# A planner that counts TensorE's instructions: gaps between pieces of 256, and a new order of every queue

## The chip, the cores and the metric

The kernel runs on one core of a Trainium2 chip. Its time is the device time of one execution in microseconds, here the median of several runs. The kernel is written with a manual schedule: the order in which each engine's instructions are emitted is the order in which that engine runs them, and engines wait for each other through semaphores.

## The reference

Two branches over 2,048 tokens of width 512 are mixed by a gate per token. Branch A is causal attention with 32 heads of 16 in four segments of 512 tokens, plus a compressed memory that each segment reads before its keys and values are added to it; branch B is a ReLU-gated feed-forward layer with an inner width of 1,792.

```python
def _A_ref(x, wq, wk, wv, wo, beta):
    ...
    for s in range(N):                       # four segments of 512 tokens
        logits = jnp.einsum('bhqd,bhkd->bhqk', qs, ks) * scale + mask
        p = _softmax(logits, axis=-1)
        a_dot = jnp.einsum('bhqk,bhkd->bhqd', p, vs)
        pq = phi(qs)
        a_mem = einsum(pq, M) / (einsum(pq, z) + 1e-06)
        outs.append(g * a_mem + (1.0 - g) * a_dot)
        M, z = M + einsum(phi(ks), vs), z + sum(phi(ks))
    return o @ wo
...
def _B_ref(x, W_gate, W_up, W_down):
    h = relu(x @ W_gate) * (x @ W_up)
    return h @ W_down
...
g = _sigmoid((x * gate_w).sum(-1, keepdims=True))
return g * a + (1 - g) * b
```

Inputs and the output are bfloat16.

## The kernel before

The work is cut into some 1,100 steps. A step is a function that emits a few instructions on one engine (or a pair of engines to choose from), with a list of the steps it comes after, a cost in microseconds, and whether it takes or gives back one of four PSUM banks (`rb`). `Plan.add` (line 125) records a step. The order of each queue is written out by hand in the list `ORDER` (line 41): each number is a step's place times five plus the engine, so it says both which engine does the step and where it stands in that engine's queue. `Plan.lay_out` (line 139) walks the five queues, always taking the queue whose next step can start first by the plan's own costs. That decides which PSUM bank a step gets and the order of emission across engines; the order within an engine is the one in `ORDER`. On TensorE it adds `SWITCH` = 0.094 us whenever the mode of tiles changes.

The steps that the text speaks of, by the letters of their names (then come the segment and other numbers):

- Q, K, V: projections of a segment, four wide matmuls each (L479, L522; for the first segment's values L505). QC, KC, VC move them out of PSUM on ScalarE or VectorE.
- QK (L738): one of nine fills of the score tile `sp` for two groups of four heads; 16 matmuls on tiles of the array, 8 for the smallest kind. EX (L749): ScalarE's exp of the whole tile into one of 11 buffers `E`; the next QK can start only when it is done, and an EX into a buffer that is still to be read waits for its reader. MK (L759): GpSimd masks the diagonal blocks of that buffer.
- PV (L786): the product with the values for one group of heads, 64 matmuls with a weight load each, once all masks of its parts are done; it takes two PSUM banks. TA, N, TB normalise and transpose the result on VectorE; OA adds the memory's part to it, on VectorE or GpSimd.
- MZ (L635): the memory's update after a segment, 64 matmuls with a weight load each; MA and MB turn it into the next memory matrix (MB on VectorE or GpSimd). MR (L681): reading the memory.
- G and U (L897): gate and up projections of one of 14 slices, four wide matmuls each. R (ReLU) and H (product) take them out.
- D and DB (L931; L855 for the last rows), W (L944; L863): the down projection in two halves of seven matmuls and the output projection into the same bank; OS scales and ST stores.
- XT, KX, MX, VS: DMA transposes and copies on SyncE's queue, beside the loads of the weights.

So TensorE's stream mixes wide matmuls (128 x 512, one weight load per matmul) with blocks of PV, MZ and QK whose matmuls use parts of the array and follow each other much faster.

Of the kernel before, what the change touches and what calls it, by code (L numbers as in the profile page):

```python
# [14 lines left out]
D = 512  # L15
# [17 lines left out]
NWARM = 19  # L33
# [68 lines left out]
]  # L102
T0, TU, SPAN, PEN_D, PEN_A, PEN_P = 19.0, 15.6, 4.1, -23.0, 150.0, 146.0


PORT = {'TG', 'RN', 'RC', 'OA', 'KO', 'MB', 'MQ', 'MN', 'GS', 'PQ', 'PK', 'N1', 'N2', 'N3', 'NM'}
PIECE = {'MK': 0.445, 'TL': 0.22, 'ZE': 0.24, 'YL': 0.22, 'MB': 0.3}


# [899 lines left out]
```

## Time and profile before

| | |
|---|---|
| median of 3 runs | 273.73 us (272.71 to 275.43) |
| the profiled execution | 274.39 us, of which 272.7 us from the first to the last instruction (the span) |
| mean granted TensorE clock | 0.994 |
| TensorE busy | 260.6 us (96%), 3,296 matmuls in the records |
| ScalarE, VectorE, GpSimd busy | 187.4, 184.9, 148.8 us |
| chain that ended last | TensorE 95%, "issue" 3%, DMA 1% |

The page gives busy times as a union per engine; "issue" is time in which the engine waited for nothing that the profile shows. The chain of work that ended last follows the end of the kernel back from releaser to releaser, and the answer in order of time lists its pieces as start, duration and what ran (L numbers are lines of the kernel before). The queue named q8 in the section on DMA queues carries instructions. Some matmul records are missing from a trace; the weight loads are complete.

### The profile page before, as it was taken

To read this page: it belongs to the slowest core of one execution; us is meant where nothing else is said; L and a number is where in the kernel's file an instruction comes from. 1 tells how busy PE (TensorE), PEld (TensorE's weight loads), DVE (VectorE), ACT (ScalarE), POOL (GpSimd) and SP (SyncE) were. 2 spreads that over 40 slices of the span, in tenths; PEclk is the share of its full clock that TensorE was granted. 3 is DMA by queue.
4 is the path that set the end of the run, shared out by engine and by line. 5 is a ranking of instruction groups with operands and counts; after the bars stand their busy time and mean duration, and the time that the engine had idled before them with its cause. 6 is when DMAs were issued, how large, how long until landed. Compare 5 with 4: busy or idle time off the path is not lost.

```text
span 272.7 us, 7949 instructions
## 1 busy us (share of the span) xinstructions
PE 260.6 (96%) x3296; PEld 124.0 (45%) x3337; DVE 184.9 (68%) x457; ACT 187.4 (69%) x179; POOL 148.8 (55%) x326
## 2 busy tenths in 40 slices
PE   8999997999899999999899997999999999999995
PEld 5444444444444544443443553544544444445463
DVE  1493685799965769768883657975695449567931
ACT  3989975679667797778576794797576576785001
POOL 7056866357889435375876555388177435343200
PEclk9999999799999999999999999999999999999999
DMA  6998346017201410000722320000100100011201
GB/s 197 286 290 211 67 149 219 4 30 93 24 19 41 117 22 2 2 19 0 121 46 60 60 59 4 19 4 18 27 2 4 59 22 2 19 22 22 19 20 59
DMA packets 33422, 16.77 MB, mean 61 GB/s; under 512 B 20074, under 2 KB 33386, under 8 KB 33386
## 3 DMA queue, kind: packets, MB, share of 16 engines
q1 hardware_dynamic: 33098, 16.00, 25.2%
q8 instruction: 26, 0.43, 0.7%
q10 hardware_dynamic: 288, 0.26, 0.3%
q14 instruction: 10, 0.08, 0.1%
HBM read 8.26 MB, written 2.10 MB: 38 GB/s over the span
## 4 chain that ended last, share of the span: by engine, by line
PE 95%; issue 3%; DMA 1%; DVE 0%; DVEq 0%
PE rb L897 37%; PE rb L931 17%; PE rb L479 10%; PE sp L738 9%; PE rb L786 7%; PE rb L944 5%; PE rb L522 4%; PE rb L505 2%; PE rb L681 1%; PE rb L855 1%; DMA xT<-in_A_x_dram 1%; PE rb L635 1%; PE rb L392 1%; PE rb L863 0%; DVE rg L874 0%
## 5 line engine op out<-in xcount | busy, mean ns | idle before, releaser
L759 POOL TENSOR_SCALAR_AFFINE_SELECT E<-E 64x256 bf16<-64x256 bf16 x256 | 113.5, 443 | 100.0 <-ACT E L749 88.3
L749 ACT ACTIVATE E<-sp 128x2048 bf16<-128x2048 f32 x72 | 135.2, 1878 | 39.6 <-PE sp L738 37.8
L897 PE MATMUL rb<-xT,wg_sb 128*128 128x512 bf16 x214 | 56.2, 387 | 0.7 <-issue 0.2
L897 PE MATMUL rb<-xT,wu_sb 128*128 128x512 bf16 x211 | 54.7, 380 | 0.6
L916 DVE TENSOR_TENSOR hT<-rb,rg 128x512 bf16<-128x512 f32 x56 | 38.0, 685 | 17.3 <-PE rb L897 13.4
L931 PE MATMUL rb<-wd_sb,hT 128*128 128x512 bf16 x201 | 48.0, 380 | 0.7 <-issue 0.3
L897 PEld LDWEIGHTS <-wg_sb 128*128 128x128 bf16 x224 | 20.9, 100 | 25.0 <-issue 5.3
L738 PE MATMUL sp<-QT,KTo 32*64 32x512 bf16 (+7 forms) x512 | 30.3, 295 | 1.7 <-issue 1.7
L897 PEld LDWEIGHTS <-wu_sb 128*128 128x128 bf16 x224 | 20.5, 98 | 24.1 <-issue 3.3
L738 PE MATMUL sp<-QT,KT 16*64 16x512 bf16 (+7 forms) x512 | 30.6, 295 | 0.0
L931 PEld LDWEIGHTS <-hT 128*128 128x128 bf16 x210 | 19.6, 98 | 23.2 <-issue 2.1
L909 ACT ACTIVATE rg<-rb 128x512 bf16<-128x512 f32 x34 | 20.0, 596 | 10.7 <-PE rb L897 5.9
L804 DVE STREAM_TRANSPOSE tA<-rb 128x512 f32<-128x512 f32 x32 | 21.2, 693 | 7.5 <-PE rb L786 7.3
L738 PEld LDWEIGHTS <-KT 16*64 16x64 bf16 x512 | 10.6, 102 | 31.4 <-issue 30.5
L911 DVE TENSOR_SCALAR rg<-rb 128x512 bf16<-128x512 f32 x22 | 15.1, 686 | 8.0 <-PE rb L897 6.9
L786 PE MATMUL rb<-E,Vs 64*32 64x448 bf16 (+7 forms) x512 | 18.6, 284 | 1.0 <-issue 1.0
L786 PE MATMUL rb<-E,Vp 64*32 64x448 bf16 (+7 forms) x512 | 17.9, 284 | 1.1 <-issue 1.1
L479 PE MATMUL rb<-xT,wq_sb 128*128 128x512 bf16 x61 | 16.2, 381 | 0.2
L479 PE MATMUL rb<-xT,wk_sb 128*128 128x512 bf16 x61 | 15.5, 380 | 0.1
L944 PE MATMUL rb<-wo_sb,oT 128*128 128x512 bf16 x57 | 14.5, 380 | 0.2
L522 PE MATMUL rb<-wv_sb,xT 128*128 128x256 bf16 (+1 forms) x96 | 14.5, 277 | 0.1
L955 DVE TENSOR_SCALAR osb<-rb,ngcol 128x512 bf16<-128x512 f32 x8 | 6.0, 750 | 12.6 <-PE rb L944 12.6
(99 smaller groups left out, 295.9 us busy)
## 6 DMA issues: line engine op xcount, KB each, us to landing
out_dram<-osb SPq DMA_DIRECT2D x15, 128.0 KB, 1.8
wd_sb<-in_B_W_down_dram SPq DMA_DIRECT2D x1, 1792.0 KB
wg_sb<-in_B_W_gate_dram SPq DMA_DIRECT2D x3, 512.0 KB, 6.2
wu_sb<-in_B_W_up_dram SPq DMA_DIRECT2D x3, 512.0 KB, 7.0
Vs<-Vp SPq DMA_DIRECT2D x8, 144.0 KB, 2.6
wk_sb<-in_A_wk_dram SPq DMA_DIRECT2D x2, 256.0 KB, 4.2
wq_sb<-in_A_wq_dram SPq DMA_DIRECT2D x2, 256.0 KB, 5.7
wo_sb<-in_A_wo_dram SPq DMA_DIRECT2D x1, 512.0 KB, 8.3
```

Source lines behind the costliest of these rows:

```text
L479: nc.tensor.matmul(rb[s.bank][:], lhsT=w[:, ci, c * P:(c + 1) * P], rhs=xT[i][:, ci, :], start=(ci == 0), stop=(ci == NC - 1))
L522: nc.tensor.matmul(rb[s.bank][:, 0:n], lhsT=xT[i][:, ci, t * P:(t + 1) * P], rhs=wv_sb[:, ci, h * D // 2:h * D // 2 + n], start=(ci == 0), ...
L738: nc.tensor.matmul(sp[64 * h:64 * h + 64, j, off:off + m], lhsT=kt[32 * j:hi, c0 + w, 64 * ck:64 * ck + 64], rhs=QT[i][32 * j:hi, c0 + w, ...
L749: nc.scalar.activation(Er[n % NE][:], sp[:], ACT.Exp, scale=SCALE)
L759: nc.gpsimd.affine_select(out=v, in_=v, compare_op=ALU.is_ge, fill=0.0, base=0, pattern=[[0, 4], [1, 64]], channel_multiplier=-1)
L786: nc.tensor.matmul(rb[s.banks[h]][32 * j:32 * j + 32, q0:q0 + m], lhsT=v[64 * h:64 * h + 64, ck // 2, o:o + 32], rhs=Er[(base + f) % NE][6 ...
L804: nc.vector.transpose(tA[k].rearrange("p b w -> p (b w)"), rb[a.banks[r]][:])
L897: nc.tensor.matmul(rb[s.bank][:], lhsT=w[:, ci, fv * P:(fv + 1) * P], rhs=xT[i][:, ci, :], start=(ci == 0), stop=(ci == NC - 1))
L909: nc.scalar.activation(rgb[k][:], rb[a.bank][:], ACT.Relu)
L916: nc.vector.tensor_tensor(hT[:, fv, :], rb[a.bank][:], rgb[k][:], ALU.mult)
L931: nc.tensor.matmul(rb[b][:], lhsT=hT[:, fv, lc:lc + P], rhs=wd_sb[:, fv, :], start=(fv == 0), stop=False)
L944: nc.tensor.matmul(rb[hold.bank][:], lhsT=oT[i][:, ci, lc:lc + P], rhs=wo_sb[:, ci, :], start=False, stop=(ci == NC - 1))
```

## The change

Each step gets a count of the instructions that it puts on TensorE. `lay_out` adds them up along TensorE's queue. At a first edge of 186 and every 256 behind it, the step that crosses the edge is stretched so that it is crossed no sooner than 5.0 us behind the moment noted for the edge ahead; that moment is when the stream was 12 instructions ahead of that edge, or 5.0 us behind the one before, if that is later. This acts only on the plan's own clock: no instruction is added for it. `ORDER` is replaced as a whole, for all five queues. The steps themselves, their tiles and their dependences are as before.

The diff without the body of `ORDER`:

```diff
 ORDER = [
...
-    135, 81, 79, 140, 160, 150, 146, 170, 166, 157, 350, 176, 375, 380, 385, 390, 355, 396, 190, 180, 360, 197, 365,
+    135, 81, 79, 140, 150, 170, 146, 160, 157, 176, 350, 167, 355, 375, 360, 365, 380, 372, 190, 180, 385, 197, 390,
...
 PORT = {'TG', 'RN', 'RC', 'OA', 'KO', 'MB', 'MQ', 'MN', 'GS', 'PQ', 'PK', 'N1', 'N2', 'N3', 'NM'}
+CODE = {'WM': 2 * NWARM, 'XP': 4, 'VI': 2, 'YP': 4, 'D': 14, 'DB': 14, 'PV': 128, 'MZ': 96}
+PAGE, PAGE0, AHEAD, FETCH = 256, 186, 12, 5.0
 PIECE = {'MK': 0.445, 'TL': 0.22, 'ZE': 0.24, 'YL': 0.22, 'MB': 0.3}
...
     def add(self, name, engines, emit, after=(), prio=0.0, lat=0.15, take=False, give=None, which=None,
-            mode="full"):
+            mode="full", code=8):
...
+        s.code = CODE.get(kind, code)
...
         gp, lock, mode, order = (0.0, 0.0, 99.0), 0.0, "full", []
+        code, edge, asked, ask = 0, PAGE0, -99.0, 0.0
...
             if e == "PE":
                 cost += SWITCH if s.mode != mode else 0.0
                 mode = s.mode
+                for i in (edge - AHEAD, edge):
+                    if code <= i < code + s.code:
+                        t = now + cost * (i - code) / s.code
+                        if i < edge:
+                            ask = t
+                        else:
+                            cost += max(0.0, asked + FETCH - t)
+                            asked, edge = max(ask, asked + FETCH), edge + PAGE
+                code += s.code
...
             mr = add(f"MR{seg}{q}", {"PE": 0.061 * len(ks)}, mrv, after=d["PQ"] + st[seg - 1]["mb"], prio=want + 4.0 * q,
-                     take=True, lat=0.25)
+                     take=True, lat=0.25, code=2 * len(ks))
...
-            a = add(f"QK{seg}{c0}{f}", {"PE": 0.262}, qk, mode="rows",
+            a = add(f"QK{seg}{c0}{f}", {"PE": 0.262}, qk, mode="rows", code=16 * len(whole[f]),
                     after=[x for w in us for x in (d["Q"][c0 + w], d["KO"][c0 + w], d["K"][c0 + w])] + fills[-1:],
                     prio=tu - 20.0, lat=0.25)
```

In the new order of TensorE every one of the 357 steps is still there, on the same engine; 317 stand at another place, the farthest 64 steps away. Of ScalarE's 178 steps 140 stay on it. In sum ScalarE has three ReLUs less and two copies, one scaling of keys and one OS more; one MB and one minimum (MN, MQ) go from GpSimd to VectorE, two OA from VectorE to GpSimd. Around the densest code the two orders read as follows (before, then after):

```
QK021 PV00 PV01 QK022             QK022 PV00 PV01 G0_13 QK023 MZ0 U0_13
QK100 MZ0 PV02 PV03 QK101         K21 PV02 PV03 QK100 D01
QK120 PV10 PV11 G1_3 QK121        QK121 PV10 PV11 MZ1 QK122
QK200 MZ1 PV12 PV13 QK201         QK200 PV12 PV13 QK201
QK221 PV20 PV21 MZ2 QK222         QK221 PV20 PV21 MZ2 QK222
QK301 PV22 PV23 QK302             QK301 PV22 PV23 QK302
QK320 PV30 PV31 G3_1 QK321        QK321 PV30 PV31 G3_2 QK322
U3_13 PV32 PV33 U3_12 D30         G3_11 PV32 PV33 U3_11 D31
```

On SyncE's queue the first gate and up pieces go out as gate 0, gate 1, up 0, up 1 instead of gate 0, up 0, gate 1, gate 2; the transposes, copies and stores behind them are moved by at most ten places.

118 rows, old and new, of the table ORDER are left out of this document.

## The prediction

> **What bounds the kernel now.** I read the page first: sections 1, 2, 3 and 4, then the chain of work that ended last in order of time, then single stretches.
>
> ```profile
> span 272.7 us, 7949 instructions
> PE 260.6 (96%) x3296; PEld 124.0 (45%) x3337; DVE 184.9 (68%) x457; ACT 187.4 (69%) x179; POOL 148.8 (55%) x326
> PEclk9999999799999999999999999999999999999999
> q8 instruction: 26, 0.43, 0.7%
> PE 95%; issue 3%; DMA 1%; DVE 0%; DVEq 0%
> ```
>
> TensorE is busy for 260.6 of 272.7 us and carries 95% of the chain; no other engine passes 69%. So only two things can shorten the kernel: TensorE's idle time, 12.1 us, and the time at a lower clock (the single 7 in the clock row). The chain shows where most of the idle time lies:
>
> ```profile
> 43.12 2.19 PE rb L786 x128
> 45.50 1.69 issue
> 47.18 0.42 PE sp L738 x15
> ...
> 68.09 0.62 PE rb L635 x64
> 68.71 2.15 PE rb L786 x125
> 70.86 0.97 issue
> 71.83 0.39 PE rb L786 x3
> ...
> 129.77 0.61 PE rb L635 x64
> 130.38 1.20 PE rb L786 x68
> 131.59 1.08 issue
> 132.67 1.14 PE rb L786 x55
> ...
> 161.11 2.16 PE rb L786 x128
> 163.28 0.59 PE rb L635 x63
> 163.86 1.44 issue
> 165.30 0.18 PE rb L635
> ```
>
> There are four gaps in which TensorE waits for nothing that the profile shows: 1.69 + 0.97 + 1.08 + 1.44 = 5.18 us. All lie inside or just behind blocks of PV (L786) and MZ (L635), the densest code there is: 64 matmuls and 64 weight loads, 128 instructions, in 1.1 us or 0.6 us. Counted in the program's own order of TensorE's instructions, what waits is number 963, 1731, 3266 (a weight load) or 3267, and 4291. These lie 768, 1536 and 1024 apart, that is 3, 6 and 4 times 256, and queue q8 moved 0.43 MB in 26 pieces, which is 6,684 instructions cut into pieces of about 256. So I read the gaps as waits for the next piece of code, with edges at 195 + 256k.
>
> **How long a piece must last.** From the edge before each gap to its end: the two PVs of the first begin 3 instructions ahead of edge 707, so 43.15 to 47.18 = 4.0 us. Edge 1475 lies 2 matmuls ahead of the end of MZ: 68.69 to 71.83 = 3.1. Edge 3011 lies 9 matmuls into MZ: 129.86 to 132.67 = 2.8. Edge 4035 lies halfway through the two PVs' row: 162.19 to 165.30 = 3.1. Two pieces went by faster without a gap worth the name:
>
> ```profile
> 100.93 0.36 PE sp L738 x16
> 101.29 2.19 PE rb L786 x127
> 103.48 0.32 PE rb L897
> ...
> 195.28 0.35 PE sp L738 x16
> 195.63 1.94 PE rb L786 x119
> 197.58 0.01 issue
> ```
>
> Their edges (2243 and 4803) lie about halfway through a QK (L738), and they lasted 2.4 and 2.1 us. In the stretch 99.0 to 102.7 the only DMA traffic is one q8 piece, in the third of 40 slices, near 99.2: ahead of the edge.
>
> ```profile
> GB/s 0 0 177 0 0 0 0 0 0 0 0 0 0 0 0 0 0 0 0 0 0 0 0 0 0 0 0 0 0 0 0 0 0 0 0 0 0 0 0 0
> q8 instruction: 1, 0.02, 1.6%
> ```
>
> So code is asked for early where the instruction stream runs ahead of the array, and not where the edge lies deep in dense code. I take 3.1 us for such edges, with 2.1 (no gap) and 4.0 as ends.
>
> The first gap has a second price, seen in three stretches (columns: us; busy of PE, PEld, DVE, ACT, POOL; clock; DMA):
>
> ```profile
> 45.00:47.70 2.70, 1.01 (x33) 0.41 (x19) 1.07 (x5) 0.10 (x2) 2.11 (x5) 1.00 0.00 1
> 47.70:51.20 3.50, 3.28 (x11) 1.41 (x10) 2.32 (x5) 2.44 (x2) 1.41 (x4) 0.51 0.02 5
> 51.20:56.00 4.80, 4.75 (x47) 2.26 (x47) 4.18 (x12) 3.54 (x3) 1.05 (x3) 1.00 0.01 2
> ```
>
> Behind it the granted clock is 0.51 for 3.5 us, so about 0.49 x 3.5 = 1.7 us are lost; behind the gaps of 1.44, 1.08 and 0.97 us it is not. [...]
>
> **The change, part by part.** Two rows more of the chain in order of time, for the durations used here:
>
> ```profile
> 26.62 0.87 PE rb L897 x4
> 28.36 0.36 PE sp L738 x16
> ```
>
> The counting itself runs when the program is written and adds no instruction. What reaches the chip is a new order of the five queues. TensorE's 3,337 matmuls and loads are the same; 151 changes between tile modes become 152, about 0.1 us by the first matmul behind one (0.32 us at 103.48 against 0.87/4 = 0.22). So the price lies in where the edges now fall.
>
> The plan counts 96 instructions for an MZ. The code loops over 4 x 4 x 4 = 64 matmuls, each with its load, and the rows agree (three MZs):
>
> ```profile
> L635 PE MATMUL rb<-Vp,pK 128*32 128x34 bf16 x192 | 2.2, 183 | 1.4 <-issue 1.4
> L635 PEld LDWEIGHTS <-pK 128*32 128x32 bf16 x192 | 1.7, 93 | 0.8 <-issue 0.8
> ```
>
> That is 128, so behind each MZ the plan's edges lie 32 instructions later against the real ones. Its first edge (186, counted from the first warm-up load, number 3 in the program) stands 6 ahead of mine; behind the first MZ it is 26 late, then about 58, then about 90. The distance that the plan keeps is kept at the wrong places for most of the run. The blocks stay: all eight pairs of PVs are still adjacent, MZ1 now follows PV10 and PV11, MZ2 still follows PV20 and PV21; only MZ0 now stands apart from any PV.
>
> I price the pieces of the new order by rows: a PV matmul 2.19/128 = 0.0171 us, an MZ 0.61, a QK of 16 matmuls 0.36, a wide matmul 0.216 (and 0.1 more behind a QK).
>
> Edge 2499 (48 PV matmuls, MZ1, QK): 0.82 + 0.61 + 0.36 = 1.79 us, so a gap of 3.1 - 1.8 = 1.3. Edge 4035 (73 of PV, 55 of MZ2): 1.25 + 0.52 = 1.77, gap 1.3. Edge 4803 (122 of PV, 6 of QK), whose edge lies just inside the first PV as at 707: 2.09 + 0.13 = 2.22, gap 0.9. Edge 1475 (109 of PV, QK, 3 of the down-projection): 1.87 + 0.36 + 0.65 = 2.88, gap 0.2. Edge 5571 (112 of PV, 4 wide, 12 of QK): 3.2, none. Edge 707 (5 wide, QK, 107 of PV): 3.3, none. All others last over 5 us. Sum 3.7 us against 5.18: a gain of 1.5. Ends: at 2.8 a piece 1.0 + 1.0 + 0.6 = 2.6; at 4.0, 2.2 + 2.2 + 1.8 + 1.1 + 0.8 + 0.7 = 8.8.
>
> Clock: the new gaps of 1.3 us are nearest to 1.44, which had no dip, yet their upper end is beyond 1.69. I take half a dip, a gain of 0.85, ends 0 and 1.7.
>
> Waits from the new order: 317 of TensorE's 357 steps stand elsewhere, and nothing in the trace prices that. TensorE's idle time apart from the gaps is 12.1 - 5.2 = 6.9 us, of which about 4.1 lie ahead of its first and behind its last matmul; 2.7 are spread. This could vanish (-2.7) or double (+2.7). I take +0.5, near zero, because the tightest loop has no less room than before: QK needs the exp of the QK ahead.
>
> ```profile
> L749 ACT ACTIVATE E<-sp 128x2048 bf16<-128x2048 f32 x72 | 135.2, 1878 | 39.6 <-PE sp L738 37.8
> PEld L738 <- ACT E L749: 0.4, 1, 0.4
> ```
>
> TensorE waited for an exp once, 0.4 us, and by my count the new order's QKs are still at least 2.5 us apart against an exp of 1.88. PV00 and PV01 move behind QK022, whose exp overwrites the E buffer that PV00 reads. That exp waits for PV00 (1.1 us), and the next QK for the exp: 0.36 + 1.1 + 0.3 + 1.88 = 3.6 us behind QK022's start, where TensorE has 0.36 + 2.19 + 0.97 = 3.5 us of other work; a wait of 0.1 at most.
>
> The other queues: in sum three ReLUs go from ScalarE to VectorE and four small steps back, one MB and one minimum go from GpSimd to VectorE, two OA the other way; all on engines that are busy for 55 to 69%; where that cover is gone, such a step costs TensorE at most its own length. On SyncE one 512 KB gate piece is issued ahead of the first up piece. At the 290 GB/s of the page's third slice that is 1.8 us later for U0_0, which two gate projections and a QK now precede (2 x 0.97 + 0.36 = 2.3); hidden, 1.8 if not. VS and the transposes move by at most ten places.
>
> ```profile
> GB/s 197 286 290 211 67 149 219 4 30 93 24 19 41 117 22 2 2 19 0 121 46 60 60 59 4 19 4 18 27 2 4 59 22 2 19 22 22 19 20 59
> ```
>
> Sum against the profiled execution, 274.39 us (0.66 above the median 273.73; span 272.7): 274.39 - 5.18 + 3.7 - 0.85 + 0.5 = 272.56, about 272.5.
>
> **The rivals.** First, the gaps shrink to those in the blocks with MZ and no dip follows: the streams run ahead at 4803 and 1475 as they did at 2243. 274.39 - 5.18 + 2.6 - 1.7 = 270.1, with nothing for other waits. For it: two of before's six short pieces had no gap. Against it: edge 4803 now lies behind the PV's own waits for two banks.
>
> Second, the change does all it says: no gap, no dip, 274.39 - 5.18 - 1.7 = 267.5. Against it: the miscount of MZ, and five pieces priced under 3.2 us.
>
> Third, slower: pieces of code arrive at the longest interval, 4.0 us, at all six edges: 274.39 - 5.18 + 8.8 + 0.5 = 278.5. It decides by 1% (over 276.5) once the gaps sum to about 6.8, an interval of some 3.7 us at all six. For it: 4.0 was measured at the edge most like the new 4803. Against it: three of the four were 2.8 to 3.1.
>
> Fourth, the gaps are not code at all but belong to the blocks, and stay: 273.7. [...] Against it: the spacing of the gaps in multiples of 256.
>
> **How the numbers follow.** My forecast has 0.50, the fourth rival 0.05, the first 0.20, the second 0.08, the slower one 0.17. A difference under 1% (271.0 to 276.5) can hardly be told from none by a measurement of this kernel. Faster: 0.20 + 0.08 + 0.02 from the forecast's lower edge = 0.30; slower 0.17; within 0.53. The range leaves out the second rival and half of the slower one: 269.2 to 277.0; the forecast's own is 271.0 to 275.5.
>
> **What would show it.** Right: gaps put down to issue ahead of instructions 2755 and 4291, each 1.0 to 2.2 us, a smaller one at 5059, none at 963; still about 26 pieces in q8; TensorE's busy time within 1 us of 260. Wrong: no gap behind MZ1 or MZ2 (pieces are asked for earlier than I think), TensorE waiting for ScalarE, VectorE or a DMA for more than 2 us in all (the new order's own waits), or gaps at instructions that are not 195 + 256k.

## The result and the profile after

The new order took 270.55 us (median of six runs, 270.51 to 271.35) against 273.15 for the kernel before (median of six, 272.71 to 275.43); the ratio is 0.9896, with an interval of 0.9861 to 0.9931. So it is faster, by about 1%. The page of its profiled execution, which took 270.55 us:

```profile
span 268.8 us, 8007 instructions
...
PE 261.6 (97%) x3337; PEld 124.0 (46%) x3337; DVE 187.4 (70%) x460; ACT 188.6 (70%) x180; POOL 146.3 (54%) x322
...
PEclk9999999999999999999999999999999999999999
...
q8 instruction: 26, 0.43, 0.7%
...
PE 90%; DVE 5%; issue 1%; DMA 1%; ACT 1%; DVEq 0%
```

The 7 in the clock row is gone, "issue" in the chain fell from 3% to 1%, and the number of code pieces is as before (26 in q8). The chain in order of time, at the places that the prediction named (lines are those of the kernel after: 799 is PV, 648 is MZ, 751 is QK, 910 a gate or up projection):

```profile
44.96 2.23 PE rb L799 x128
47.20 0.97 PE rb L910 x4
...
102.44 1.15 PE rb L799 x64
...
105.84 0.89 DVE o L828 x2
106.74 0.04 issue
106.78 1.90 PE rb L910 x8
...
160.05 2.16 PE rb L799 x128
162.21 0.51 PE rb L648 x53
162.72 0.87 issue
163.59 0.25 PE rb L648 x10
...
189.35 2.19 PE rb L799 x128
191.54 0.21 PE sp L751 x5
191.75 0.32 issue
```

The first pair of PVs now passes its edge (963) without a gap. Behind MZ2 a gap of 0.87 us stands ahead of instruction 4291, and one of 0.32 ahead of 5059. The gap expected ahead of 2755 does not look like one: at 102.44 the chain leaves TensorE and runs through VectorE. The list of TensorE's waits shows why (columns: us in total, times, longest):

```profile
PE rb L910 <- DVE o L828: 1.2, 1, 1.2
PE rb L395 <- DVE zeros L267: 1.0, 1, 1.0
PE rb L648 <- issue: 0.9, 1, 0.9
PE rb L405 <- DMA xT<-in_A_x_dram: 0.6, 1, 0.6
PE sp L751 <- issue: 0.3, 1, 0.3
```

A gap of 1.21 us from 105.56 ahead of a wide matmul is put down to VectorE. The weight load that is late there is instruction 2754 in the program's order, one short of an edge, just as 3266 was one short of 3267 before. The profile named the engine whose semaphore came last; the experiments below show that it was the edge. So the gaps are 1.21 + 0.87 + 0.32 = 2.40 us, where before they were 5.18.

### The profile page after: what moved, and what is told of

The parts are those of the page before. It is cut to its first block, busy times and chain, and to the rows that moved or that the text cites. A ratio compares the mean times of both kernels' runs of the same rounds, so it can differ in the third digit from the quotient of the medians.

```text
span 268.8 us, 8007 instructions
## 1 busy us (share of the span) xinstructions
PE 261.6 (97%) x3337; PEld 124.0 (46%) x3337; DVE 187.4 (70%) x460; ACT 188.6 (70%) x180; POOL 146.3 (54%) x322
## 4 chain that ended last, share of the span: by engine, by line
PE 90%; DVE 5%; issue 1%; DMA 1%; ACT 1%; DVEq 0%
PE rb L910 33%; PE rb L944 17%; PE rb L492 10%; PE sp L751 9%; PE rb L799 6%; PE rb L957 5%; PE rb L535 4%; PE rb L518 2%; PE rb L868 1%; PE rb L694 1%; DMA xT<-in_A_x_dram 1%; DVE pqT L571 1%; DVE hT L929 1%; ACT E L762 1%; PE rb L405 1%
## 5 line engine op out<-in xcount | busy, mean ns | idle before, releaser
L910 PE MATMUL rb<-xT,wu_sb 128*128 128x512 bf16 x224 | 56.7, 380 | 0.0
L944 PE MATMUL rb<-wd_sb,hT 128*128 128x512 bf16 x210 | 49.0, 379 | 0.0
L910 PEld LDWEIGHTS <-wg_sb 128*128 128x128 bf16 x224 | 20.3, 98 | 26.5 <-issue 5.6
L751 PE MATMUL sp<-QT,KTo 32*64 32x512 bf16 (+7 forms) x512 | 30.9, 295 | 0.3 <-issue 0.3
L922 ACT ACTIVATE rg<-rb 128x512 bf16<-128x512 f32 x31 | 18.5, 597 | 9.3 <-PE rb L910 7.4
L924 DVE TENSOR_SCALAR rg<-rb 128x512 bf16<-128x512 f32 x25 | 16.9, 680 | 4.8 <-PE rb L910 4.6
L799 PE MATMUL rb<-E,Vs 64*32 64x448 bf16 (+7 forms) x512 | 18.0, 284 | 0.0
L957 PE MATMUL rb<-wo_sb,oT 128*128 128x512 bf16 x60 | 15.1, 379 | 0.0
L828 DVE TENSOR_TENSOR o<-tA,co 128x256 bf16<-128x256 f32 x32 | 14.4, 474 | 0.1
L390 DVE CAST KT<-rb 128x512 bf16<-128x512 f32 x10 | 6.9, 689 | 10.8 <-PE rb L492 10.4
```

Of the source, the lines that this page charges most:

```text
L751: nc.tensor.matmul(sp[64 * h:64 * h + 64, j, off:off + m], lhsT=kt[32 * j:hi, c0 + w, 64 * ck:64 * ck + 64], rhs=QT[i][32 * j:hi, c0 + w, ...
L799: nc.tensor.matmul(rb[s.banks[h]][32 * j:32 * j + 32, q0:q0 + m], lhsT=v[64 * h:64 * h + 64, ck // 2, o:o + 32], rhs=Er[(base + f) % NE][6 ...
L910: nc.tensor.matmul(rb[s.bank][:], lhsT=w[:, ci, fv * P:(fv + 1) * P], rhs=xT[i][:, ci, :], start=(ci == 0), stop=(ci == NC - 1))
L922: nc.scalar.activation(rgb[k][:], rb[a.bank][:], ACT.Relu)
L924: nc.vector.tensor_scalar(rgb[k][:], rb[a.bank][:], 0.0, None, ALU.max)
L944: nc.tensor.matmul(rb[b][:], lhsT=hT[:, fv, lc:lc + P], rhs=wd_sb[:, fv, :], start=(fv == 0), stop=False)
```

## The experiments

Code theory: TensorE's gaps are waits for the next piece of 256 instructions, and what the change gained is where the edges of these pieces now fall. Order theory: the gaps belong to the blocks of PV and MZ, and the new order gained by other waits. One part of the change needed no run: the new planner with the old list emits, on all five engines, the same instructions in the same order as before. The counting by itself does nothing on the chip.

**Moving the edges alone.** Instructions without use, put at the front, move every later edge against the work and leave its order as it is. First they went into the warm-up, with 111 small matmuls for 19 wide ones (a shift of 184 instructions), 147 (a shift of 256, so every edge is back where it was) and 35 (a shift of 32):

```diff
-            for k in range(n):
-                nc.tensor.matmul(rb[3][:, 0:P], lhsT=zeros[:], rhs=zeros[:], start=True, stop=True)
+            for k in range(111):
+                j = 32 * (k % 4)
+                nc.tensor.matmul(rb[3][j:j + 32, 0:32], lhsT=zeros[:, 0:32], rhs=zeros[:, 0:32], start=True, stop=True,
+                                 tile_position=(0, j), skip_group_check=True)
```

The order of before, shifted by 184:

> The order of before, with 92 small matmuls and their loads more in the warm-up (each narrower, so the warm-up should take about as long as it did): nothing else moves, but every edge of 256 instructions falls 184 instructions earlier in the stream. Code theory (the gaps wait for pieces of code, the gain of the change is where the edges fall): the gaps at 963, 1731, 3267 and 4291 vanish, one of about 1.3 us appears at instruction 3339 of the old count, behind the first matmuls after PV13; no stretch at half clock; 269 to 270 us, with up to 1 us more if the warm-up costs more. Order theory (the gaps belong to the blocks of PV and MZ, and the new order gains by other waits): four gaps as before, 273 to 274.5 us.

Measured: 273.12 us, ratio to before 0.9965 (0.9921 to 1.0009). In time it gained nothing, against the 269 to 271 us of code theory, but its chain is what code theory said (lines two further than before's):

```profile
128.24 0.61 PE rb L637 x61
128.85 1.76 PE rb L788 x100
130.62 2.33 issue
132.95 0.74 PE rb L788 x19
```

The four gaps are gone and one stands ahead of instruction 3522, which is 3338 of the old count; 2.33 us instead of 1.3. A stretch at half clock follows it in this execution (columns as in the prediction's stretches):

```profile
134.00:137.50 3.50, 3.28 (x16) 1.30 (x10) 1.89 (x5) 1.88 (x1) 1.44 (x4) 0.51 0.04 7
```

Six of its ten runs had a mean clock of 0.994 or less, as this one. The warm-up also cost more than I allowed: the first exp starts at 16.7 us instead of 14.1, and TensorE was slow for longer (four wide matmuls took 1.91 us at 9.41, against 1.03 us at 7.71 in the kernel before). The four runs at full clock took 270.98 to 271.37.

> The order of before with 128 small matmuls and loads more in the warm-up, so that all edges fall on the same instructions as in before. Code theory: the four gaps of before stand at the same instructions, 273 to 274 us (up to 1 us more for the warm-up). Order theory: the same. If it came out faster like the shift by 184, the warm-up and not the edges would be the cause.

Measured: 274.95 us, ratio 1.0027 (0.9981 to 1.0073). The gaps are back at instructions 1219, 1987, 3522 and 4547, which are 963, 1731, 3266 and 4291 plus 256, with 1.60, 0.84, 1.38 and 1.17 us. So the long warm-up is not what removed them.

> The new order with every edge 184 instructions earlier by the same means. Code theory: the gaps at 2755, 4291 and 5059 vanish, one of about 1.0 us stands at instruction 2571 of the old count; 269.2 us, 268.5 to 270.2. Order theory: 270.5 to 271.5 us, gaps where they were.

Measured: 269.40 us, ratio 0.9856 (0.9808 to 0.9905). No gap is left behind any PV or MZ, not even the one of 1.0 us that I expected, although the first exp starts 3.1 us later than in the new order.

> The new order with every edge 32 instructions earlier, a bad place by the same count: gaps expected at 1699, 2723, 4259, 5027 and 5795 of the old count, in sum about 1.8 us more than in the new order. Code theory: 272.3 us, 271.3 to 274 with a stretch at half clock if one of the gaps is over 1.5 us. Order theory: 270.5 to 271 us.

Measured: 271.08 us, ratio 0.9920 (0.9884 to 0.9956). A miss in size, below the 271.3 to 274 us expected: the gaps sum to 1.00 + 0.81 + 0.78 = 2.6 us, about as much as without the shift. The pieces that end at 1699 and 5027 of the old count lasted about 2.2 us each by the rows of the chain and had no gap. But the gap that the profile had given to VectorE moved with the edge, and is now put down to issue, ahead of a QK:

```profile
102.03 2.16 PE rb L801 x128
104.19 0.61 PE rb L650 x64
104.80 1.00 issue
105.81 0.42 PE sp L753 x16
```

That QK is another instruction of another step, and the edge is what the two have in common.

**The same shift without the longer warm-up.** Here the 92 small matmuls stand ahead of the first QK, and the warm-up is as it was:

```diff
             def qk(e, s, f=f):
+                if seg == 0 and c0 == 0 and f == 0:
+                    for k in range(92):
+                        nc.tensor.matmul(sp[32 * (k % 4):32 * (k % 4) + 32, 0, 0:32], lhsT=zeros[:, 0:32], rhs=zeros[:, 0:32],
+                                         start=True, stop=True, tile_position=(0, 32 * (k % 4)), skip_group_check=True)
```

> The order of before with its warm-up untouched; 92 small matmuls with their loads stand ahead of the first QK instead, so every later edge falls 184 instructions earlier. They cost at most 0.9 us of TensorE themselves. Code theory: none of the four gaps of before, one of 1.3 to 2.4 us behind instruction 3338 of the old count, so 5.2 - 1.9 - 0.9 = 2.4 us less than before (1.9 to 3.0), about as fast as the new order, and 1.7 us more in executions with a stretch at half clock behind that gap. Order theory: before's time plus up to 0.9 us.

Measured: 271.59 us, ratio 0.9935 (0.9899 to 0.9972). Again one gap alone:

```profile
126.01 0.61 PE rb L635 x64
126.62 1.74 PE rb L790 x100
128.36 2.64 issue
131.00 0.74 PE rb L790 x19
```

Its five runs at full clock took 270.59 to 271.48, the five at 0.994 or less 271.69 to 273.60. So the old order, untouched, comes within about 1 us of the new one as soon as its edges fall elsewhere.

> The new order with the same 92 small matmuls ahead of the first QK. Code theory: the gaps of 1.21, 0.87 and 0.32 us go, as they did with the longer warm-up, and up to 0.9 us is paid for the extra matmuls: 1.0 to 2.0 us less than the new order, 268.6 to 269.6. Order theory: 270.6 to 271.5.

Measured: 268.20 us (267.63 to 268.47), ratio 0.9791 (0.9733 to 0.9849): faster than the new order by 2.35 us (2.04 by the new order's repeat, below), where the gaps were 2.40. They were timed at different times, but the kernel before took nearly the same beside each (273.07 us here, 273.15 and 273.59 beside the new order). No gap stands behind a PV or an MZ, and the first exp starts no later (14.2 us against 14.3), so the extra matmuls cost nothing that shows. The gate projection that the new order's profile had waiting for VectorE's product (DVE o) starts here at 106.03 us, while that product begins only at 106.29; so it does not wait for it, and the 1.21 us were the edge's. This is the fastest version found.

```profile
span 266.6 us, 8152 instructions
...
PEclk9999999999999999999999999999999999999999
```

> The new order with 128 small matmuls and loads, one whole piece, ahead of the first QK: 36 more than in the kernel that took 268.2 us, and every later edge is back on the instruction where the new order has it. Code theory: the gaps behind MZ1, MZ2 and at the end of PV13 return with 2 to 2.7 us in sum; 270.5 to 271.3, over 2 us slower than with 92. If the extra matmuls themselves were what helped, it would take 268 to 268.6.

Measured: 275.11 us, ratio 1.0043 (1.0006 to 1.0080). With 36 matmuls more the gaps return at the three instructions of the new order (0.89, 1.56 and 0.28 us in its trace), as code theory has it. The time is far above what I expected, for a reason I had not seen: 256 dense instructions hold a whole piece themselves.

```profile
13.01 1.12 PE sp L749 x128
...
14.87 1.89 PE rb L914 x8
16.76 2.31 issue
19.07 1.01 PE rb L914 x2
```

The gap of 2.31 us ahead of instruction 451 is an edge, and half clock follows in the next stretch:

```profile
18.70:22.20 3.50, 3.13 (x22) 0.88 (x22) 0.00 (x0) 1.47 (x1) 0.14 (x1) 0.51 0.93 222
```

Seven of its ten runs had a mean clock of 0.994 or less, as this one. That gap and the half clock cost some 4.0 us; with the 2.7 us of the three returned gaps this takes 268.2 to 274.9. As a control of the time it is spoilt; as one of the places it is clear.

**Moving work alone.** In the new order, MZ1 and MZ2 were put behind the next QK, with one wide step between the PVs and that QK (PV10 PV11 G1_6 QK122 MZ1, and PV20 PV21 K32 QK222 MZ2), by the numbers in the list alone.

> The new order with four steps moved: MZ1 and MZ2 no longer follow their PVs but stand behind the next QK, with one wide step moved between PVs and QK, as MZ0 stands in the new order. Code theory: the gaps at 2755 and 4291 shrink from 1.21 and 0.87 to at most 0.4 each, two more changes of tile mode cost 0.1 to 0.3 each, the gap at 5059 stays: 1.2 to 1.8 us less, 268.8 to 269.4. Order theory: no gain, 270.3 to 271.5, since VectorE's queue reaches MA before MZ now and the steps behind it wait.

Measured: 270.47 us, ratio 0.9876 (0.9825 to 0.9927), no gain over the new order. The gap at 2755 is gone and the one at 4291 fell to 0.17, but the waits of TensorE show what came in their place:

```profile
PE rb L910 <- DVE mzacc L660: 0.8, 2, 0.4
PE sp L751 <- issue: 0.7, 1, 0.7
PE rb L492 <- DVE tA L817: 0.6, 1, 0.6
PE rb L535 <- DVE tA L817: 0.4, 1, 0.4
```

VectorE's list still has MA early, so it waits for the late MZ, and the transposes behind it free the banks late: 1.8 us of waits for banks where 1.9 us of gaps went, and the gap at 5059 grew from 0.32 to 0.70. Here the order theory named the right mechanism.

In the order of before, with the 92 matmuls ahead of the first QK, one step moved (PV12 D11 PV13 instead of PV12 PV13 QK201 D11):

> The order of before with the 92 small matmuls ahead of the first QK and one step moved: D11 stands between PV12 and PV13 instead of behind QK201, so that the one piece that held dense code alone gets a wide step of 1.5 us. Code theory: the gap of 2.64 us shrinks to 0 to 1.3, no stretch at half clock; 268.5 to 270.2, the old order as fast as the new one or faster. Order theory: the old order stays above 271.5, and the moved step makes PV13 wait for a bank.

Measured: 271.07 us (270.38 to 271.11), ratio 0.9898 (0.9848 to 0.9949), mean clock 0.999 or more in all four runs. The gap fell to 1.41, but the later QK made its exp, and the next QK, late by 1.1 us:

```profile
129.81 0.53 PE rb L790 x38
130.34 1.41 issue
...
132.62 0.40 PE sp L742 x16
...
133.11 1.89 ACT E L753
```

**The disputed cost by itself.** 1,024 small matmuls and their loads, eight pieces of code, behind the last step of the new order, on a bank that nothing else uses any more:

> The new order with 1,024 small matmuls and loads, 8 pieces of code, behind its last step, on a free bank: dense code with nothing to wait for. Code theory: a piece needs about 1.1 us of the array but 2.8 to 4.0 us pass from edge to edge, with a gap put down to issue at every 256th instruction. Order theory: no gaps, about 1.1 us a piece, 9 us in all.

Measured (one execution, 294.22 us):

```profile
264.86 1.83 PE rb L994 x213
266.69 2.54 issue
269.23 1.21 PE rb L994 x128
270.44 2.52 issue
272.96 1.22 PE rb L994 x120
274.18 2.23 issue
276.41 1.23 PE rb L994 x117
277.64 2.50 issue
```

Every 128 matmuls with their loads, 1.2 us of work, are followed by a gap of 2.2 to 2.5: 3.45 to 3.8 us from edge to edge, in seven of seven. The profile shows nothing that TensorE waits for there, and from 266 to 292 us q8 moves seven packets, one for each gap. The clock records of this execution give half clock from 270.24 us to the end (mean 0.962), but the first gap, 2.54 us, came ahead of that, so the gaps are no effect of the lower clock.

Beside the last two runs the new order was timed once more:

> The new order itself beside the two others. Both theories: 270.5 us, 269.6 to 271.4, gaps of 0.8 to 1.3 us at 2755 and 4291 and a smaller one at 5059, no stretch at half clock.

Measured: 270.24 us (269.88 to 270.50), ratio 0.9871 (0.9812 to 0.9930), gaps of 1.25 and 1.01 us at 2755 and 4291, none over 0.15 at 5059 and 0.24 at 1731.

Of the two theories the code theory holds for where the gaps are and for what the change gained. Without gaps the two orders should be about equal: 268.2 for the new one, 271.2 - 2.6 = 268.6 for the old one by its median run at full clock and its one gap. The last number is argued; the run that was to show it (D11 moved) got a new wait instead.

## Why the prediction was right, and where its sizes were off

The measured 270.55 us lies in the range of 269.2 to 277.0, but below the forecast's own 271.0 to 275.5 and 2.0 us under the number given, 272.5. It is the outcome of the first rival (270.1), to which I gave 0.20. The mechanism was right; that the range held is owed to its taking in a rival. The terms one by one.

The bound and the edges: right. The edges at 195 + 256k, read from four gaps, held in every kernel and moved with the shifts as they should. (The 6,684 instructions are the new order's count; the old order has two semaphore instructions more. Nothing hangs on it.)

The miscount of MZ and the places: right. Gaps came ahead of 2755, 4291 and 5059 and of none of the old four but 4291. That the planner keeps its distance at the wrong places is my reason why 2.40 us of gaps are left. It fits that 184 instructions at the front take them away: 184 earlier is, modulo 256, 72 later, and I had the plan's edges 58 to 90 late behind MZ1 and MZ2. But no kernel with the right count was timed, so this is argued, not shown.

The size of the gaps is the term that was off: 3.7 us predicted, 2.40 measured. The lengths of the pieces were priced well (1.79, 1.77 and 2.22 us; the rows give 1.79, 1.75 and 2.30). The step that failed is "I take 3.1 us for such edges": counted the same way, the three intervals were 3.0, 2.6 and 2.6, the first inside before's four (2.8 to 4.0), the other two below them. The later runs show how loosely an interval is fixed: by the rows of the chains, from 2.2 us without a gap in the new order shifted by 32 to 4.9 at the gap of the kernel with D11 moved. I had also expected a gap of 0.2 at 1731; it was too small to see, 0.24 in the repeat.

The clock: I took half a dip, the new order had none in ten runs. The reason given, that gaps of 1.3 us are nearest to 1.44, held, and should have been followed all the way. The runs bear out a tie between these gaps and the clock. Sorted by the longest gap that the kernel has at an edge, so many runs had a mean clock of 0.994 or less: none of 31 up to 1.4 us; 3 of 10 at 1.6 us (the old order shifted by 256); 15 of 46 at 1.69 us (before's runs beside the experiments); 18 of 30 at 2.3 to 2.6 us. Beside the second set of runs, before's median was 272.8 at full clock and 274.6 with a dip.

The waits from the new order: +0.5 taken. The span fell by 272.7 - 268.8 = 3.9 us, the gaps and the dip account for 2.78 + 1.7 = 4.5, so the rest is +0.6. The start is part of it (0.61 us ahead of the first transposes instead of 0.20).

So the sum with measured terms is 274.39 - 5.18 + 2.40 - 1.7 + 0.6 = 270.5, which closes by construction, as the 0.6 is what was left. Of the 2.05 us between it and 272.56, 1.3 are the gaps and 0.85 the clock; the waits make up for 0.1. That is near the first rival's number, for about the first rival's reason, shorter gaps and no dip; it had two gaps of 1.3 us behind the MZs and none at 5059, and there were 1.21, 0.87 and 0.32. The second rival (no gap at all) is what the shifted new order shows, not the change itself. The third needed 4.0 us at all edges and got 2.6 to 3.0. The fourth, that the gaps belong to the blocks, fell with the shifts: the same blocks in the same order lose or gain their gaps with the edges. In the dense tail, which holds no such block, each crossing brought a gap of 2.2 to 2.5 us.

Two of the signs came out otherwise than I had them. The gap at 4291 was 0.87 us, under the 1.0 named. And TensorE's waits for VectorE and DMA add up to 2.8 us, over the 2 us that I had called a sign of being wrong; 1.2 of them are the edge at 2755, and 1.0 is the wait for the zeros at the start, which the kernel before has too. TensorE's busy time (261.6 us with all matmuls in the records, 259.0 in the repeat with 38 missing) could decide nothing to within 1 us.

## What to carry to other kernels

Where TensorE's gaps have no releaser, count its instructions in the program's order and take the numbers modulo 256, the spacing measured here: equal remainders pointed to late code in this kernel (963, 1731, 3267 and 4291 all leave 195), and shifting the stream by useless instructions at a free place tested it without touching the order. The gaps moved with the shifts, so do not tune around one of them without looking at all the edges behind it; here 184 useless instructions took 2.0 to 2.35 us off the new order, which itself had taken 2.6 off the old one. And a step moved in one queue must be moved in the queues that wait for it, or the gap can come back as a wait for a bank: 1.8 us of such waits for 1.9 us of gaps with MZ1 and MZ2 moved.

## What the runs showed of the hardware that I had not expected

In the dense tail 256 instructions of TensorE took 3.45 to 3.8 us from edge to edge, with 1.2 us of work. In the seven gaps of that tail the packet in q8 starts 1.0 to 1.6 us after the edge before, takes 0.9 to 1.2 us, and TensorE goes on 1.2 to 1.5 us after it has ended. A gap of this kind can also be booked under another engine, as the 1.21 us under VectorE were. And a single gap of 1.69, 2.31 or 2.33 us was followed by half clock for some 3.4 us in the traces above (0.51 in stretches of 3.50 us), while other executions of the same kernels had none; much of the spread of the kernel before goes with it (272.8 us at full clock, 274.6 with a dip).

The clock records of the two main traces have one thing more. In that of the kernel before, the first record of full clock lies 6.80 us into the span; the clock halves 40.96 us behind it and is full again after 3.413 us, and 40.96 is 12 times 3.413. In that of the new order, full clock begins at 7.18 us and ends 262.83 us later, behind the span; that is 77 times 3.413. Why the same gap brings a dip in some executions only, no run shows.
